# One start-up constant, the warming products and the unread products of a four-segment attention and feed-forward kernel

## The chip, the cores and the metric

The kernel runs on one core of one Trainium2 chip. Its time is the device time of one execution in microseconds (us). Five engines work side by side, each in its own order: TensorE (PE in the profile, its weight loads PEld), VectorE (DVE), ScalarE (ACT), GpSimd (POOL) and SyncE (SP, which issues most DMAs).

## The reference

The input x has 2048 rows of 512. Four layers follow each other: attention, feed-forward, attention, feed-forward, twice with the same weights, each added to x after a normalization.

```python
x = x + _A_ref(_layernorm(x), wq, wk, wv, wo, beta)
x = x + _B_ref(_layernorm(x), w_gate, w_up, w_down)
x = x + _A_ref(_layernorm(x), wq, wk, wv, wo, beta)
x = x + _B_ref(_layernorm(x), w_gate, w_up, w_down)
```

`_A_ref` has 32 heads of 16 columns and cuts the rows into 4 segments of 512. In a segment each head does a causal softmax attention (`a_dot`) and reads a memory matrix `M` with a normalizer `z` (`a_mem`), which gather phi(k) v and phi(k) over the earlier segments; phi(t) is t + 1 above zero and exp(t) below. The two are mixed by a gate for each head:

```python
g = sigmoid(beta).reshape(1, H, 1, 1)        # beta: 32 numbers
o = g * a_mem + (1.0 - g) * a_dot
```

`_B_ref` is `gelu(x @ w_gate) * (x @ w_up) @ w_down` with 1792 inner columns.

## The kernel before

The work is eight pieces, k = 0 to 7: four segments in each of the two attention layers, each with its feed-forward piece. All of x and all weights stay in SBUF. Rows lie on the 128 partitions, four tiles of 128 rows to a segment; the normalized rows are turned (`xnT`) by DMA transposes or, for some pieces, by TensorE transposes against an identity, and an engine evicts the turned tile from PSUM. Scores are computed with keys on the partitions, exponentiated by ScalarE (L1396) into one of ten slots `pt`, masked by GpSimd (L1343, L1348) or VectorE (L1353), and multiplied with the values (the flush, L954). The memory's update multiplies the turned `phik` with the values, and VectorE adds it to `macc` (L895).

The order of all instructions on all engines is written out by the kernel itself: `order` runs a model of the engines (`Clocks`, with a duration for each step) and emits each instruction where the model finds its inputs ready. TensorE's turn goes first to score rounds, then to an item (a group of products for one of the 8 PSUM banks). Where nothing is ready while scores are still to come, it emits an unread product of `warm`, a tile of ones, into a free bank: 128 weights by 512 columns, one instruction (through `product`, L476), or four with 32 weights each where the array is in its column tiling (L471). These are called fills here. The model counts each as `Clocks.MM[512]`, 0.2158 us. The fills beside some transposes (L584, 256 columns) are another piece of code.

The start is written by hand. Four tiles of x are loaded, two by SyncE's queue and two by ScalarE's, then beta on ScalarE's queue, spread to all 128 partitions (`beta_bc`, L315); SyncE loads the weights. TensorE begins with `WARM` unread products of 128 x 512 (`keep_warm`, L349), which keep it busy until the first data is there. The four tiles are normalized (VectorE L544) and turned by TensorE (`first_turn`, L596); ScalarE evicts the first two (L599), VectorE the other two (L601). Then follow the first k products (`first_k`, L909), two groups of q products (`first_q`, L914), the second k products, and their evictions (L1228, L1231, L1237 on ScalarE, L1234 on VectorE), and the first scores (L938).

From beta come two constants, exp(beta) in `tmp_e` (a corner of `macc`) and exp(-beta) in `tmp_e2`, both by ScalarE, which in its order stand after the statistics of the fourth tile and ahead of the evictions of L599:

```python
nc.scalar.activation(out=tmp_e, in_=beta_bc[:], func=ACT.Exp)                 # L1202
nc.scalar.activation(out=tmp_e2[:], in_=beta_bc[:], func=ACT.Exp, scale=-1.0) # L1203
```

VectorE adds one to each (`gate_constants`, L389, L391) after the eviction of L1234.

Of the kernel before, what the change touches and what calls it, by code (L numbers as in the profile page):

```python
# [11 lines left out]
ACT = mybir.ActivationFunctionType  # L12
# [3 lines left out]
BF16 = mybir.dt.bfloat16  # L16
I32 = mybir.dt.int32

P = 128
D = 512  # L20
H = 32
# [12 lines left out]
EPS_LN = 1e-5  # L34
EPS_MEM = 1e-6
MANUAL = {ENG.PE, ENG.Activation, ENG.SP, ENG.DVE, ENG.Pool}
WARM = 15
UNIT = 256
ROUNDS = 9
STEPS = KT * ROUNDS  # L40
# [17 lines left out]
BANKS = 8  # L58
# [227 lines left out]
def order(pol, nc, cst, seg, wrk, psp, A_x, A_wq, A_wk, A_wv, A_wo, A_beta, B_x, B_w_gate, B_w_up, B_w_down, out):  # L286
# [12 lines left out]
    wu_sb = cst.tile([P, KT, FF], BF16, name="wu_sb")  # L299
    wd_sb = cst.tile([P, FT, D], BF16, name="wd_sb")  # L300
    gel_sb = cst.tile([P, FT, L], BF16, name="gel_sb")
    beta_bc = cst.tile([P, H], BF16, name="beta_bc")

    def load(dst, src):
        nc.sync.dma_start(out=dst, in_=src)
# [6 lines left out]

    for j in range(TPS):
        (nc.scalar if j % 2 else nc.sync).dma_start(out=x_sb[:, j, :], in_=xv[:, j, :])
    nc.scalar.dma_start(out=beta_bc[:], in_=A_beta.partition_broadcast(P))  # L315
    for cols in (slice(0, D // 2), slice(D // 2, D)):
        load(w_att["k"][:, :, cols], w_view(A_wk)[:, :, cols])
        load(w_att["q"][:, :, cols], w_view(A_wq)[:, :, cols])
# [19 lines left out]
    warm = cst.tile([P, P], BF16, name="warm")  # L338
    wide = warm[:].unsqueeze(1).to_broadcast([P, 4, P])
# [4 lines left out]
    ps_all = psp.tile([P, BANKS, L], F32, tag="ps", bufs=1, name="ps")  # L344
    pt_all = wrk.tile([P, PT_SLOTS, 4, UNIT], BF16, tag="pt", bufs=1, name="pt")

    def keep_warm(n, bank):
        for _ in range(n):
            nc.tensor.matmul(ps_all[:, bank, :], lhsT=warm[:], rhs=wide, start=True, stop=True)  # L349

    keep_warm(WARM, 0)

# [23 lines left out]
    tmp_e2 = cst.tile([P, H], F32, name="tmp_e2")  # L376
    cden = cst.tile([P, H], BF16, name="cden")
    macc = cst.tile([P, 4, P], F32, name="macc")
    tmp_e = macc[:, 0, 0:H]
# [85 lines left out]
    def product(out, lhsT, rhs, start=True, stop=True):  # L465

        if ck.mode == "columns" or ck.mode == "rows" and (any(it.kind == "flush" and it.near() for it in items)):
            ck.tiling("columns")
            for c in range(4):
                r = slice(32 * c, 32 * c + 32)  # L470
                nc.tensor.matmul(out[r], lhsT=lhsT[:, r], rhs=rhs, start=start, stop=stop, tile_position=(0, 32 * c))  # L471
            ck.count += 4
        else:
            ck.tiling("whole")
            ck.count += 1
            nc.tensor.matmul(out, lhsT=lhsT, rhs=rhs, start=start, stop=stop)  # L476
# [722 lines left out]
    nc.scalar.activation(out=spare[:, 1, :], in_=x_sb[:, TPS - 1, :], func=ACT.Square, scale=root, bias=shift[:],  # L1199
                         accum_out=n0.mv[:, TPS - 1, 1:2])  # L1200

    nc.scalar.activation(out=tmp_e, in_=beta_bc[:], func=ACT.Exp)  # L1202
    nc.scalar.activation(out=tmp_e2[:], in_=beta_bc[:], func=ACT.Exp, scale=-1.0)  # L1203

    first_stats(0)
    first_stats(1)
# [14 lines left out]
    half = L // 2  # L1221
    n0.first_turn(0)
    n0.first_turn(1)
    n0.first_turn(2)
    n0.first_turn(3)
    ps1 = ps_all[:, 1, :]
# [47 lines left out]
    def next_e():  # L1274
        if not e_slots.free or e_slots.queue or phase[0] is not None:
            return
        now = streams[0][0] + streams[0][1] / STEPS if streams else 1e9
        act = ck.act
        idle = act.free <= ck.pe and act.table == "exp" and not act.only and not any(j[0] <= ck.pe and not j[4] for j in act.jobs)
        got = [j for j in e_jobs if j[1] <= ck.pe and j[2]() and (idle or j[0] <= now)]  # L1280
        if got:
            job = min(got, key=lambda j: j[0])
            e_jobs.remove(job)
            job[3](job[1], pol.e_slack)
            ck.serve()
# [17 lines left out]
    def tight():  # L1303

        return any(slot_free[slot_of(k, t)] is None for k, t in streams[2:4])
# [7 lines left out]
    def rounds_now(idle=False):  # L1313

        if not streams or phase[0] is not None and phase[1] > pol.hold or not rounds_ready(2):
            return 0
        n, left = len(free_pairs()), len(streams)
        wait = backlog()
        if n >= 2 and (idle or left <= 4 or wait < (pol.early if streams[0][0] < 1 else pol.starve)):
            return 2  # L1320
        return 0

    def pick():

        got = [i for i in range(BANKS) if banks[i] <= ck.pe]
        if not got:
            return None
        mine = sum(banks[i] > ck.pe for i in range(BANKS) if i not in score_banks)
        if streams and mine >= pol.cap and backlog() < pol.near and rounds_ready(2):
            return None  # L1330
        apart = {i for i in range(BANKS) if i not in score_banks and banks[i] > ck.pe + pol.soon} if streams else ()
        return min(got, key=lambda i: (-len(pairs_of(set(range(BANKS)) - {i, *apart})), banks[i]))

    def open_item(got, bank):
        it = min(got, key=lambda it: it.due())
        items.remove(it)
        it.ps.bank = bank
        banks[bank] = 1e9
        return it
# [83 lines left out]
    while streams or items or opened or ck.busy():  # L1423
        assert ck.pe < 2000.0, (streams[:1], [(it.kind, it.due()) for it in items[:9]], e_jobs[:2], banks)
        pol.move(ck.pe)
        ck.dve.shun = pol.shun
        ck.serve()
        next_e()
        n = rounds_now()
        if n:  # L1430
            score(n)
            continue
        if opened:
            cost, fn = opened.ops.pop(0)
            fn()
            ck.on_pe(cost)
            if not opened.ops:
                it, opened = opened, None
                it.done()
            continue  # L1440
        bank = pick()
        if bank is not None:
            late = ck.pe - pol.flush_wait
            for ck.back in (pol.lag, 0.0):
                got = [it for it in items if it.after in ev and it.ready() and (
                    it.kind != "flush" or not streams or tight() or it.posted < late or ck.mode == "columns")]
                if got:
                    break
            ck.back = 0.0
            if got:  # L1450
                opened = open_item(got, bank)
                continue

        n = rounds_now(True)
        if n:
            score(n)
            continue
        if bank is not None:
            if streams:
                ps = Psum()  # L1460
                ps.bank = bank
                product(ps(), warm[:], wide)
                ck.on_pe(Clocks.MM[512])
                ps.read(ck.pe)
                ck.fills.append(ck.pe)
                continue
        ck.pe += 0.05
        ck.stalls.append(ck.pe)
# [3 lines left out]
@with_exitstack  # L1472
def kernel(
    ctx: ExitStack,
    tc: tile.TileContext,
    A_x: bass.AP,
    A_wq: bass.AP,
    A_wk: bass.AP,
    A_wv: bass.AP,
    A_wo: bass.AP,  # L1480
    A_beta: bass.AP,
    B_x: bass.AP,
    B_w_gate: bass.AP,
    B_w_up: bass.AP,
    B_w_down: bass.AP,
    out: bass.AP,
):
    cst = ctx.enter_context(tc.tile_pool(name="cst", bufs=1))
    seg = ctx.enter_context(tc.tile_pool(name="seg", bufs=1))
    wrk = ctx.enter_context(tc.tile_pool(name="wrk", bufs=2))  # L1490
    psp = ctx.enter_context(tc.tile_pool(name="psp", bufs=1, space=bass.MemoryType.PSUM))
    ctx.enter_context(tc.manual_schedule(engines=MANUAL))
    order(Policy(POLICY, CHANGES), tc.nc, cst, seg, wrk, psp, A_x, A_wq, A_wk, A_wv, A_wo, A_beta, B_x, B_w_gate, B_w_up, B_w_down, out)
# [31 lines left out]
```

## Time and profile before

| what | value |
|---|---|
| time, median of 3 runs | 546.05 us (546.04 to 547.07) |
| the profiled execution | 545.75 us, span 544.0 us |
| TensorE busy | 531.3 us, 98% of the span |
| VectorE, ScalarE, GpSimd busy | 82%, 80%, 56% |
| mean granted TensorE clock | 0.999 |
| unread products at the start (L349) | 15 |
| fills (L476 and L471) | 19 instructions and 48 instructions |

The span runs from the first to the last instruction; the time has some work around it. In rows of the timeline the columns are start, duration, engine, line, operation, out<-in, count, and in brackets how long the engine was idle before and what ended that. A row of the chain of waits has start, duration and the work. In a table of stretches stand the bounds, the length, the busy time with the number of instructions, the granted TensorE clock, the DMA share and GB/s. The ends of matmuls are modelled, so a short idle time of TensorE can be hidden in the tail of the product before it.

### The profile page before, as it was taken

Reading aid. Unit: us, or ns where it says so; the run is one execution under the profiler, and the core shown is the slowest. Engines: PE = TensorE matmul, PEld = TensorE weight load, DVE = VectorE, ACT = ScalarE, POOL = GpSimd, SP = SyncE. Lnnn points to the kernel's source line nnn. Section 1 sums busy time; section 2 is a strip of 40 time slices with the busy share of each in tenths; the row PEclk is TensorE's granted clock in tenths of the full one; section 3 lists DMA queues with packets and bytes.
Section 4 is the critical chain, followed back from the end, with each engine's and each line's share of the span. In section 5 each row is a group of like instructions: output and inputs, shape, how many; then the busy total and the mean of one; then the engine's idle time right before and its main releaser. Section 6 shows DMA issues by size and latency. Waiting matters only on the chain.

```text
span 544.0 us, 21276 instructions
## 1 busy us (share of the span) xinstructions
PE 531.3 (98%) x9273; PEld 276.3 (51%) x9334; DVE 443.7 (82%) x816; ACT 434.7 (80%) x540; POOL 305.5 (56%) x359
## 2 busy tenths in 40 slices
PE   8999999999999999999999999999999999999997
PEld 4454555454545444554545555545465456555444
DVE  6998999799988999779987998889586797786342
ACT  5999989988898989989899798996879977920330
POOL 4898786369746788339993468716753265300000
PEclk9999999999999999999999999999999999999999
DMA  8406511610331123310312250221320114100001
GB/s 249 117 13 192 118 20 13 176 33 22 45 56 21 26 40 58 44 40 7 41 32 49 33 72 3 41 32 23 78 52 3 22 21 82 24 3 22 19 0 40
DMA packets 64926, 26.95 MB, mean 50 GB/s; under 512 B 49216, under 2 KB 64832, under 8 KB 64832
## 3 DMA queue, kind: packets, MB, share of 16 engines
q1 hardware_dynamic: 64400, 25.31, 22.6%
q8 instruction: 73, 1.20, 0.9%
q10 hardware_dynamic: 432, 0.27, 0.2%
q14 instruction: 21, 0.17, 0.1%
HBM read 9.71 MB, written 2.10 MB: 22 GB/s over the span
## 4 chain that ended last, share of the span: by engine, by line
PE 88%; DVE 7%; DMA 2%; issue 2%; ACT 0%; ACTq 0%; SPq 0%; DVEq 0%
PE ps L476 46%; PE ps L471 26%; PE ps L938 8%; PE ps L954 7%; DVE st L514 1%; DVE x_sb L1027 1%; DMA beta_bc<-in_A_beta_dram 1%; DVE byq L971 1%; PE ps L586 1%; DVE phiq L745 1%; PE ps L584 1%; DMA phik<-e 0%; DMA amT<-am 0%; DVE xn L544 0%; DVE e L764 0%
## 5 line engine op out<-in xcount | busy, mean ns | idle before, releaser
L1396 ACT ACTIVATE pt<-ps 128x1024 bf16<-128x1024 f32 x288 | 278.9, 1025 | 44.6 <-PE ps L938 41.1
L1343 POOL TENSOR_SCALAR_AFFINE_SELECT pt<-pt 128x256 bf16<-128x256 bf16 (+1 forms) x192 | 107.0, 571 | 118.0 <-ACT pt L1396 112.0
L1092 DVE TENSOR_TENSOR gel_sb<-gel_sb,ps 128x512 bf16<-128x512 bf16 x112 | 75.3, 682 | 33.9 <-PE ps L476 25.0
L476 PE MATMUL ps<-xnT,wu_sb 128*128 128x512 bf16 x287 | 66.8, 379 | 1.4 <-issue 1.1
L476 PE MATMUL ps<-xnT,wg_sb 128*128 128x512 bf16 x261 | 62.6, 379 | 0.9 <-issue 0.5
L764 POOL TENSOR_SCALAR e<-e 128x512 bf16<-128x512 bf16 x37 | 57.9, 1565 | 1.8 <-ACT e L741 0.7
L971 DVE STREAM_TRANSPOSE byq<-ps 128x512 f32<-128x512 f32 x64 | 45.0, 706 | 16.5 <-PE ps L954 15.9
L476 PE MATMUL ps<-wd_sb,gel_sb 128*128 128x512 bf16 (+1 forms) x293 | 56.8, 340 | 1.3 <-issue 1.0
L1348 POOL TENSOR_SCALAR_AFFINE_SELECT pt<-pt 64x1024 bf16<-64x1024 bf16 x40 | 47.8, 1196 | 15.0 <-ACT pt L1396 13.7
L1027 DVE TENSOR_TENSOR x_sb<-x_sb,ps 128x512 bf16<-128x512 bf16 (+1 forms) x68 | 42.8, 640 | 16.3 <-PE ps L476 14.7
L471 PE MATMUL ps<-wd_sb,gel_sb 128*32 128x512 bf16 (+1 forms) x792 | 47.1, 378 | 0.3 <-issue 0.3
L476 PEld LDWEIGHTS <-wu_sb 128*128 128x128 bf16 x301 | 28.2, 98 | 33.8 <-issue 0.7
L471 PE MATMUL ps<-xnT,wg_sb 128*32 128x512 bf16 x700 | 42.4, 380 | 0.0
L514 DVE BATCH_NORM_STATS2 st<-x_sb 128x6 f32<-128x512 bf16 x60 | 40.4, 674 | 0.4 <-DMA x_sb<-in_A_x_dram 0.3
L476 PEld LDWEIGHTS <-wg_sb 128*128 128x128 bf16 x273 | 25.3, 98 | 28.8 <-issue 0.2
L476 PEld LDWEIGHTS <-gel_sb 128*128 128x128 bf16 x306 | 28.3, 98 | 22.7 <-issue 1.1
L954 PE MATMUL ps<-pt,vaug 128*32 128x256 bf16 (+2 forms) x1344 | 34.6, 238 | 0.0
L417 POOL TENSOR_SCALAR kx<-kf,masks 128x512 bf16<-128x512 bf16 x20 | 33.5, 1678 | 1.2
L471 PE MATMUL ps<-xnT,wu_sb 128*32 128x512 bf16 x588 | 34.1, 379 | 0.0
L1151 ACT ACTIVATE gel_sb<-gel_sb 128x2048 bf16<-128x2048 bf16 (+1 forms) x21 | 33.2, 1643 | 0.0
L544 DVE TENSOR_SCALAR xn<-x_sb,mv,rs 128x512 bf16<-128x512 bf16 x58 | 31.3, 592 | 2.2 <-POOL rs L532 1.9
L954 PEld LDWEIGHTS <-vaug 128*32 128x32 bf16 x1344 | 27.8, 97 | 10.4 <-issue 2.2
(147 smaller groups left out, 883.6 us busy)
## 6 DMA issues: line engine op xcount, KB each, us to landing
vz<-vaug SPq DMA_DIRECT2D x14, 136.0 KB, 2.9
wg_sb<-in_B_w_gate_dram SPq DMA_DIRECT2D x8, 224.0 KB, 4.6
wu_sb<-in_B_w_up_dram SPq DMA_DIRECT2D x8, 224.0 KB, 4.3
wd_sb<-in_B_w_down_dram SPq DMA_DIRECT2D x7, 256.0 KB, 4.2
x_sb<-in_A_x_dram SPq DMA_DIRECT2D x3, 512.0 KB, 7.3
out_dram<-x_sb SPq DMA_DIRECT2D x12, 128.0 KB, 1.8
xnT<-xn SPq DMA_TRANSPOSE x40, 2.5
wk_sb<-in_A_wk_dram SPq DMA_DIRECT2D x2, 256.0 KB, 6.0
```

The lines of the kernel that those rows point to most:

```text
L471: nc.tensor.matmul(out[r], lhsT=lhsT[:, r], rhs=rhs, start=start, stop=stop, tile_position=(0, 32 * c))
L476: nc.tensor.matmul(out, lhsT=lhsT, rhs=rhs, start=start, stop=stop)
L514: nc.vector.bn_stats(out=self.st6[:, 0, :], in_=x_sb[:, self.tt0 + j, :])
L764: lambda eng: eng.tensor_scalar(out=e[0][:], in0=e[0][:], scalar1=1.0, scalar2=None, op0=ALU.min), summed)
L938: nc.tensor.matmul(ps_all[:, bank, o + c0:o + c0 + n], lhsT=lhsT, rhs=self.q[rows, b, q0:q0 + n], start=True, stop=True, tile_position=(32 ...
L954: nc.tensor.matmul(ps()[32 * j:32 * j + 32, q0:q0 + n], lhsT=va[:, ki * VW + g:ki * VW + g + 32], rhs=pt_all[:, places[i], j, c0:c0 + n], ...
L971: nc.vector.transpose(out=self.byq[:, par, :, :].rearrange("p a c -> p (a c)"), in_=ps()[:])
L1027: ck.dve.post(ck.made(), slack, (0.15 + 0.00104 * (c1 - c0), lambda: nc.vector.tensor_tensor(out=xt, in0=xt, in1=ps()[:, 0:c1 - c0], op=AL ...
L1092: ck.dve.post(ck.made(), NORMAL, (0.683, lambda: nc.vector.tensor_tensor(out=g, in0=g, in1=ps()[:], op=ALU.mult), lambda t: (ps.read(t), e ...
L1343: nc.gpsimd.affine_select(out=view, in_=view, pattern=[[0, 4], [0, n], [1, C]], compare_op=ALU.is_ge, fill=0.0, base=C, channel_multiplier=-1)
L1348: nc.gpsimd.affine_select(out=view, in_=view, pattern=[[0, 4 * TPS], [1, C]], compare_op=ALU.is_ge, fill=0.0, base=0, channel_multiplier=-1)
L1396: nc.scalar.activation(out=pt_all[:, s0:s0 + 2, 2 * p:2 * p + 2, :].rearrange("p r h c -> p h r c"), in_=ps_all[:, pair[0]:pair[1] + 1, :] ...
```

## The change

Beta is loaded as one row of 32 numbers in one partition. After the second tile's transposes, TensorE multiplies that row with one row of ones into the last PSUM bank, so that all 128 partitions get it, and ScalarE takes both exponentials from PSUM, now after the two evictions of L599 in its order. The warming products are 12 and not 15. A fill has 128 columns and not 512; the model of the engines still counts it as 512 columns, so that the order of all instructions and their banks stays what it was.

```diff
-WARM = 15
+WARM = 12
...
-    beta_bc = cst.tile([P, H], BF16, name="beta_bc")
+    beta_row = cst.tile([1, H], BF16, name="beta_row")
...
-    nc.scalar.dma_start(out=beta_bc[:], in_=A_beta.partition_broadcast(P))
+    nc.scalar.dma_start(out=beta_row[:], in_=A_beta.partition_broadcast(1))
...
-    nc.scalar.activation(out=tmp_e, in_=beta_bc[:], func=ACT.Exp)
-    nc.scalar.activation(out=tmp_e2[:], in_=beta_bc[:], func=ACT.Exp, scale=-1.0)
...
     n0.first_turn(0)
     n0.first_turn(1)
+    beta_ps = ps_all[:, BANKS - 1, 0:H]
+    nc.tensor.matmul(beta_ps, lhsT=warm[0:1, :], rhs=beta_row[:], start=True, stop=True)
+    nc.scalar.activation(out=tmp_e, in_=beta_ps, func=ACT.Exp)
+    nc.scalar.activation(out=tmp_e2[:], in_=beta_ps, func=ACT.Exp, scale=-1.0)
     n0.first_turn(2)
     n0.first_turn(3)
...
             if streams:
                 ps = Psum()
                 ps.bank = bank
-                product(ps(), warm[:], wide)
+                product(ps()[:, 0:P], warm[:], wide[:, 0, :])
                 ck.on_pe(Clocks.MM[512])
```

## The prediction

> **What bounds the kernel now.** I read the page first: how full the engines are, and which of them the chain that ended last runs through.
>
> ```profile
> span 544.0 us, 21276 instructions
> PE 531.3 (98%) x9273; PEld 276.3 (51%) x9334; DVE 443.7 (82%) x816; ACT 434.7 (80%) x540; POOL 305.5 (56%) x359
> PE 88%; DVE 7%; DMA 2%; issue 2%; ACT 0%; ACTq 0%; SPq 0%; DVEq 0%
> ```
>
> TensorE bounds the kernel and every other engine follows it, so a change must shorten a stretch in which TensorE itself is late. The edit touches two places: the start, and wherever unread products lie. For the start I read the chain of waits in order of time, then the timeline of the same microseconds.
>
> ```profile
> 1.71 5.38 DMA beta_bc<-in_A_beta_dram
> 7.09 0.02 issue
> 7.11 0.23 ACT macc L1202
> 7.34 0.12 ACT tmp_e L1203
> 7.46 0.98 ACT xnT L599 x2
> 8.44 0.04 issue
> 8.48 0.60 PE ps L909 x4
> ...
> 1.11 4.79 PE L349 MATMUL ps<-warm 128*128 128x512 bf16 x15 [1.11 <-DVE warm L340]
> 4.01 1.39 PEld L349 LDWEIGHTS <-warm 128*128 128x128 bf16 x7 [0.22 <-issue]
> 6.63 0.72 PE L596 MATMUL ps<-ident,xn 128*128 128x128 bf16 x8 [0.73 <-DVE xn L544]
> 7.16 0.73 DVE L544 TENSOR_SCALAR xn<-x_sb,mv,rs 128x512 bf16<-128x512 bf16 x2 [0.21 <-POOL rs L1193]
> 7.37 1.06 ACT L599 ACTIVATE xnT<-ps 128x512 bf16<-128x512 bf16 x2
> 7.63 0.72 PE L596 MATMUL ps<-ident,xn 128*128 128x128 bf16 x8 [0.29 <-DVE xn L544]
> 9.12 0.38 ACT L1228 ACTIVATE wd_sb<-ps 128x256 bf16<-128x256 f32 x1 [0.68 <-PE ps L909]
> 10.99 3.77 ACT L1396 ACTIVATE pt<-ps 128x1024 bf16<-128x1024 f32 x4 [0.18 <-PE ps L938]
> ```
>
> The chain begins with the load of beta. ScalarE's queue holds the two exponentials of beta ahead of the evictions of the first two turned tiles (L599), beta lands at 7.09, and the first k products (L909) wait for those evictions. Nothing needs beta so early; it is only queued first.
>
> For the unread products I read the groups that read `warm`, one row per form.
>
> ```profile
> L471 PE MATMUL ps<-warm x48: 377/379/380, 73.8 to 135.7; 128*32 128x512 bf16 x48
> L476 PE MATMUL ps<-warm x19: 376/379/390, 21.8 to 140.1; 128*128 128x512 bf16 x19
> ```
>
> An L471 product is four instructions side by side, so there are 48/4 + 19 = 31 fills, all between 21.8 and 140.1 us; for the last 400 us the kernel has none.
>
> **The change, part by part.** *Beta.* What leaves ScalarE's path is the wait for beta and the two exponentials. The next latest thing is TensorE's own turning. The first eight transposes (two tiles) run from 6.63 to 7.35; the second tile needs the second xn, so the first tile is done about 7.03. The evictions take 1.06 / 2 = 0.53 each and a little more for one alone: first from about 7.08, second from the end of the transposes at 7.35, or from 7.56 when ScalarE is free, to about 8.13 (now 7.37 + 1.06 = 8.43). But L909 also stands behind the fourth tile's transposes in TensorE's order: their xn is there at 7.16 + 0.73 = 7.89, four transposes at the pitch of 0.056 (below) issue from about 7.96 to 8.18. So L909 starts at about 8.20 and not at 8.48: **-0.28 us**.
>
> The product for beta goes between the second and the third tile's transposes, in TensorE's gap before 7.63, where it waits for xn. It has 32 columns and one row; its nearest row, a 128-column transpose, costs 0.056, so it hides unless beta lands after 7.5. Its load is one row instead of 128 on the same queue behind the same two x tiles, so I take 7.09 as the latest landing. Waiting behind it would be the third and fourth transposes, and everything after. The two exponentials now read PSUM, a form the trace lacks: between 0.12 (the chain's step for the second) and 0.38 each (L1228, eight times as wide, from PSUM). They stand after the evictions, at 8.13, and end by 8.4 to 8.9; the next in ScalarE's queue, L1228, can start only at 9.12 - 0.28 = 8.84, since it waited 0.68 for TensorE. I take nothing, with +0.05 as the bad end; without that cover it would be 0.2 to 0.8.
>
> *Warming.* Three products at the full-clock pitch: the last seven weight loads take 1.39, so (1.39 - 0.10) / 6 = 0.215 each, 0.65 in all. They end near 5.25 instead of 5.90, ahead of the first xn, for which TensorE already waits. Time: nothing; what it may cost is the clock (rivals).
>
> *Fills.* The pitch of 128 columns, and the fills with what surrounds them:
>
> ```profile
> 20.86 1.06 PE L586 MATMUL ps<-ident,xn 128*128 128x128 bf16 x16
> 21.31 1.62 ACT L462 ACTIVATE xnT<-ps 128x512 bf16<-128x512 bf16 x3
> 21.75 0.59 PE L476 MATMUL ps<-warm 128*128 128x512 bf16 x2
> ...
> 70.97 0.81 PE L476 MATMUL ps<-warm 128*128 128x512 bf16 x3
> 71.95 0.42 PEld L476 LDWEIGHTS <-phik 128*128 128x128 bf16 x7 [0.23 <-DMA phik<-e]
> ...
> 73.82 1.47 PE L471 MATMUL ps<-warm 128*32 128x512 bf16 x24
> 75.51 1.37 POOL L1343 TENSOR_SCALAR_AFFINE_SELECT pt<-pt 128x512 bf16<-128x512 bf16 x2
> 75.55 1.47 PE L476 MATMUL ps<-warm 128*128 128x512 bf16 x6
> 76.95 0.63 PE L954 MATMUL ps<-pt,vaug 128*32 128x256 bf16 x24
> ...
> 79.98 0.81 PE L476 MATMUL ps<-warm 128*128 128x512 bf16 x3
> 80.30 0.60 ACT L462 ACTIVATE xnT<-ps 128x512 bf16<-128x512 bf16 x1
> 81.29 1.89 PE L476 MATMUL ps<-xnT,wg_sb 128*128 128x512 bf16 x7
> ...
> 112.69 0.38 PE L476 MATMUL ps<-warm 128*128 128x512 bf16 x1
> 114.24 0.69 DVE L895 TENSOR_TENSOR macc<-macc,ps 128x512 f32<-128x512 f32 x1 [0.15 <-PE ps L476]
> ...
> 134.59 1.47 PE L471 MATMUL ps<-warm 128*32 128x512 bf16 x24
> 136.83 0.23 PEld L586 LDWEIGHTS <-xn 128*128 128x128 bf16 x4 [0.40 <-DVE xn L544]
> ```
>
> Sixteen transposes in 1.06 with a tail of 0.22 give a pitch of 0.84 / 15 = 0.056; six fills in 1.47 with a tail of 0.38 give 0.218. A cut fill saves 0.16, and 31 of them 5.0 us of TensorE time. A fill, though, stands where the order had nothing ready, so I ask at each group what the next real product waits for.
>
> - At 21.75, two fills: the v product needs the first eviction of 21.31, which lands about 21.9 (0.60 for one, as at 80.30); from 22.18 it can move to about 22.05. ScalarE has no idle time there. Between 0 and -0.13; I take -0.05.
> - At 70.97, three: the next products wait for the transposed phik at 71.95. Zero.
> - At 73.82 and 75.55, twelve: the flush at 76.95 needs the masks, which GpSimd ends at 75.51 + 1.37 = 76.88. The fills are long enough to hide in that; the 12 x 0.16 = 1.9 us become idle time. Zero.
> - At 79.98, three and one more before the gate products at 81.29: these need the eviction that ends at 80.90. Up to 81.29 - 80.95 = 0.34; ScalarE is busy here too, so I take half, -0.15.
> - At 112.69, one: the update behind it releases L895, for which VectorE waited 0.15. Up to -0.15; I take -0.07.
> - At 134.59, six: the transposes behind wait for xn, 0.40. Zero. The last three fills near 139 to 140 give at most 3 x 0.16 = 0.48 and probably a third of one; -0.05.
>
> After 141 us nothing changes any more, and what has been won up to there stays won.
>
> Sum: -0.28 - 0.05 - 0.15 - 0.07 - 0.05 = **-0.60 us**; by the ends of the terms from about -0.25 to -1.35. The profiled execution took 545.75 (544.0 and 1.75 around it), 0.30 under the median of 546.05; against the median I forecast 546.05 - 0.6 = **545.45**.
>
> **The rivals.** *The clock falls at the start (slower).* The granted clock in stretches of 3.41 us, and just after the last:
>
> ```profile
> 3.94:7.35 3.41, 2.67 (x17) 1.00 0.78 212
> 539.83:543.24 3.41, 1.04 (x10) 1.00 0.14 39
> 543.20:543.40 0.20, 0.00 (x0) 0.61 0.00 0
> ...
> 8.92 1.04 PE L914 MATMUL ps<-xnT,wq_sb 128*128 128x256 bf16 x8
> 9.79 0.60 PE L909 MATMUL ps<-xnT,wk_sb 128*128 128x256 bf16 x4
> ```
>
> A stretch busy for 1.04 of 3.41 (30%) ended with the clock cut; one busy for 2.67 (78%) did not. With three products fewer the latter falls to 2.67 - 0.65 = 2.02 (59%). If the clock is cut for less than some share between 59% and 78%, it is cut at 7.35 for one stretch, to 10.77. Price: sixteen products of 256 columns, pitch (1.04 - 0.27) / 7 = 0.11; at half clock from about 8.5 ten of them are done by 10.77, six more take 0.66, so they issue until 11.4, where now the last group ends its issue at 9.79 + 0.44 = 10.23. That is +1.2 against before; less the 0.32 of the fills, 546.05 + 0.9 = **546.9**. Stretches with the cut fills could fall too: twelve of them leave 3.41 - 1.9 = 1.5 (44%) if a stretch begins at 73.7; that would push it beyond 547.2. For it: two of the edits take activity away. Against it: 59% is far from 30%.
>
> By the Trainium skill, "TensorE: Matmul & The Clock Gate", Part 1, the clock is halved only after a whole idle window of about 3.4 us; by that nothing would fall here, and the sum would stand. The trace does not bear it out exactly: the clock went at 543.2 at the end of a stretch that was 30% busy. Part 4 of the same page says that transposes do not count as activity in the same way; by that the first stretch is emptier than its busy time, which makes this rival likelier.
>
> *The fills pass whole (faster).* The chain of waits counts TensorE through the fills at 73.8 to 76.95. If my reading of the masks is wrong and the flush can move, up to 1.9 us more come out: 545.45 - 1.9 = **543.6**. Against it: 76.88 and 76.95 fit too well.
>
> *Beta still holds the start (no change).* If the one-row load lands no earlier and TensorE, not ScalarE, now stands at it past 7.6, the 0.28 is lost again and what remains is the fills: **545.7**, or 546.0 if those are absorbed as well.
>
> **How the numbers follow.** My forecast 0.58, the clock 0.20, the fills whole 0.10, beta 0.12. A measurement of this kernel can tell about 0.2% (1.1 us) from no change, so faster means under 544.95 and slower over 547.15. Faster: the fills whole, 0.10, and the far end of my terms, 0.10, together 0.20. Slower: the half of the clock's chance in which more than one stretch falls, or the fills give nothing back, 0.10, and 0.05 for a stall that I have not seen: 0.15. Within: 0.65. The range runs from my terms' good end, 546.05 - 1.35 = 544.7, to one fall of the clock with little from the fills, 547.0; beyond lie the fills whole and a second fall.
>
> **What would show it.** Right: the two L599 evictions begin near 7.1 and L909 near 8.2; the exponentials of beta stand between them and L1228, which waits for TensorE and not for them; L938's first scores start near 10.3 instead of 10.56. The flush now at 76.95 waits idle for GpSimd, and the update's phik still ends the wait near 71.7. The granted clock is 1.00 from 4 to 543 us. Wrong: a granted clock of half anywhere between 7 and 15 or 73 and 82 us, shown as a doubled pitch of L909 and L914; a wait of TensorE for beta ahead of the third tile's transposes; a time under 544.7 or over 547.0.

## The result and the profile after

| | before | changed |
|---|---|---|
| median of 11 runs | 545.86 us (545.50 to 547.07) | 544.78 us (544.50 to 545.29) |
| ratio | | 0.9978, 95% interval 0.9971 to 0.9986 |
| span of the profiled execution | 544.0 us | 543.0 us |

The change makes the kernel 0.22% faster, some 1.1 us, where 0.6 were forecast. The page of the changed kernel:

```profile
span 543.0 us, 21272 instructions
PE 527.9 (97%) x9271; PEld 276.1 (51%) x9332; DVE 443.4 (82%) x816; ACT 434.5 (80%) x540; POOL 306.4 (56%) x359
PE 83%; DVE 11%; issue 2%; DMA 2%; ACT 1%; POOL 0%; SPq 0%; ACTq 0%; DVEq 0%
```

TensorE lost 3.4 us of work but the span only 1.0 us, and 4% of the chain went to VectorE: most of what was cut is now waiting time. The start, from the chain of waits (start, duration, what) and then from the timeline of the changed kernel:

```profile
1.23 3.00 DMA x_sb<-in_A_x_dram
...
7.40 0.72 PE ps L596 x8
8.12 0.44 PE ps L909 x4
...
3.23 1.29 DVE L1183 BATCH_NORM_STATS2 st<-x_sb 128x6 f32<-128x512 bf16 x2 [0.60 <-DMA x_sb<-in_A_x_dram]
6.83 1.08 ACT L599 ACTIVATE xnT<-ps 128x512 bf16<-128x512 bf16 x2 [1.01 <-PE ps L596]
7.05 0.18 PE L1223 MATMUL ps<-beta_row,warm 1*128 1x32 bf16 x1
7.80 0.20 ACT L1224 ACTIVATE macc<-ps 128x32 f32<-128x32 f32 x1
7.97 0.60 PE L909 MATMUL ps<-xnT,wk_sb 128*128 128x256 bf16 x4
8.60 0.38 ACT L1230 ACTIVATE wd_sb<-ps 128x256 bf16<-128x256 f32 x1 [0.51 <-PE ps L909]
```

Beta has left the chain, which now begins with a tile of x. The evictions (L599) start right behind the transposes, the product for beta (L1223) stands in a gap, its exponentials end before TensorE has work for L1230, which waits 0.51 for TensorE. The first k products start at 7.97, not at 8.48: 0.51 earlier, of which VectorE's first statistics, at 3.23 and not at 3.45, make 0.22.

The places of the fills in the timeline:

```profile
73.07 0.64 PE L471 MATMUL ps<-warm 128*32 128x128 bf16 x24
74.22 0.40 PE L938 MATMUL ps<-q,kf 16*128 16x64 bf16 x10 [0.37 <-ACT pt L1398]
74.54 0.51 PE L476 MATMUL ps<-warm 128*128 128x128 bf16 x6
74.82 1.38 POOL L1345 TENSOR_SCALAR_AFFINE_SELECT pt<-pt 128x512 bf16<-128x512 bf16 x2
74.98 0.51 PE L954 MATMUL ps<-pt,vaug 128*32 128x256 bf16 x16
75.84 0.30 PE L954 MATMUL ps<-pt,vaug 128*32 128x64 bf16 x8 [0.34 <-POOL pt L1345]
...
79.96 1.24 PE L476 MATMUL ps<-xnT,wg_sb 128*128 128x512 bf16 x4
...
108.85 2.37 SPq L437 DMA_TRANSPOSE phik<-e  x1
112.37 0.96 PE L476 MATMUL ps<-vaug,phik 128*128 128x128 bf16 x13 [0.41 <-DMA phik<-e]
113.44 0.69 DVE L895 TENSOR_TENSOR macc<-macc,ps 128x512 f32<-128x512 f32 x1 [0.49 <-PE ps L476]
```

The flush (L954) begins at 74.98, while the two masks run until 74.82 + 1.38 = 76.20, and goes on at 75.84, when only the first of them is done: asked for alone, the row is a mask of 128x512 that takes 0.97, until 75.79, and a shorter one of 128x256 that ends at 76.20. The gate products moved from 81.29 to 79.96. At 112 us the shorter fill only lengthens the wait for the turned phik.

To see where time was won I compare the same exponentiations of scores (288 of them, in the same order) in the profiled executions: how much earlier (-) or later (+) one starts than in the profile before, in us. The column heads are its start before.

| kernel | 11.0 | 29.2 | 70.1 | 78.5 | 86.8 | 114.8 | 169.9 | 470.3 |
|---|---|---|---|---|---|---|---|---|
| changed | -0.52 | -0.69 | -0.69 | -0.99 | -1.13 | -0.80 | -1.06 | -1.01 |
| changed, once more | -0.39 | -0.56 | -0.56 | -0.85 | -0.99 | -0.32 | -1.21 | -0.84 |
| fills alone | -0.18 | -0.35 | -0.35 | -0.64 | -0.79 | -0.60 | -0.86 | -0.52 |
| twelve fills alone | -0.13 | -0.13 | -0.13 | -0.42 | -0.42 | +0.17 | -0.44 | -0.14 |
| all but these twelve | -0.39 | -0.56 | -0.57 | -0.45 | -0.60 | -0.30 | -0.57 | -0.32 |
| start alone | -0.43 | -0.44 | -0.44 | -0.41 | -0.41 | +0.04 | -0.08 | +0.11 |
| beta alone | -0.14 | -0.15 | -0.15 | +0.08 | +0.08 | +0.48 | +0.37 | +0.36 |
| warming alone | -0.29 | -0.29 | -0.29 | +0.09 | +0.08 | +0.27 | +0.15 | -0.01 |

From one column to the next a row shows what that stretch gave. One execution has chance in it: where DMAs end the wait (near 72, 112 and 400 us) the rows move by some tenths whatever was edited.

### The profile page after: what moved, and what is told of

It reads as the page before. It is cut to its first block, busy times and chain, and to the rows that moved or that the text cites. A ratio compares the mean times of both kernels' runs of the same rounds, so it can differ in the third digit from the quotient of the medians.

```text
span 543.0 us, 21272 instructions
## 1 busy us (share of the span) xinstructions
PE 527.9 (97%) x9271; PEld 276.1 (51%) x9332; DVE 443.4 (82%) x816; ACT 434.5 (80%) x540; POOL 306.4 (56%) x359
## 4 chain that ended last, share of the span: by engine, by line
PE 83%; DVE 11%; issue 2%; DMA 2%; ACT 1%; POOL 0%; SPq 0%; ACTq 0%; DVEq 0%
PE ps L476 44%; PE ps L471 25%; PE ps L938 7%; PE ps L954 6%; DVE st L514 2%; DVE x_sb L1027 1%; DVE xn L544 1%; DVE byq L971 1%; DMA phik<-e 1%; DVE phiq L745 1%; DMA x_sb<-in_A_x_dram 1%; DVE mv L522 1%; DMA amT<-am 0%; DVE e L745 0%; ACT pt L1398 0%
## 5 line engine op out<-in xcount | busy, mean ns | idle before, releaser
L1345 POOL TENSOR_SCALAR_AFFINE_SELECT pt<-pt 128x256 bf16<-128x256 bf16 (+1 forms) x192 | 108.3, 577 | 116.5 <-ACT pt L1398 110.6
L954 PE MATMUL ps<-pt,vaug 128*32 128x256 bf16 (+2 forms) x1344 | 34.8, 238 | 0.3 <-POOL pt L1345 0.3
L954 PEld LDWEIGHTS <-vaug 128*32 128x32 bf16 x1344 | 27.9, 97 | 10.5 <-issue 2.3
```

The source lines that it names most:

```text
L954: nc.tensor.matmul(ps()[32 * j:32 * j + 32, q0:q0 + n], lhsT=va[:, ki * VW + g:ki * VW + g + 32], rhs=pt_all[:, places[i], j, c0:c0 + n], ...
L1345: nc.gpsimd.affine_select(out=view, in_=view, pattern=[[0, 4], [0, n], [1, C]], compare_op=ALU.is_ge, fill=0.0, base=C, channel_multiplier=-1)
```

## The experiments

All ratios are to the kernel before, run on the same chip in the same rounds; each row of the table above belongs to one of these kernels.

**Beta alone.**

```diff
-WARM = 12
+WARM = 15
-                product(ps()[:, 0:P], warm[:], wide[:, 0, :])
+                product(ps(), warm[:], wide)
```

> The kernel before with the beta part alone (one row, product, exponentials behind the two evictions); 15 warming products and 512-column fills stay. Theory 'landing' (the 128 small rows of beta delay the x tiles; without them the first normalized tile is there 0.23 us sooner, and the queue order gives the other 0.29): VectorE's first statistics at about 3.23 instead of 3.45, first k products at about 7.97 instead of 8.48, the whole start and the end 0.5 us earlier, 545.4. Rival 'chance' (tiles land 0.2 us earlier or later from one execution to the next, whatever is loaded): statistics near 3.45, first k products near 8.20, 0.3 us in all, 545.6. Rival 'clock' (the earlier start came from fewer warming products): first k products after 8.3, no gain.

Measured: 546.04 us, ratio 1.0000 (0.9991 to 1.0009). Its timeline:

```profile
3.60 1.29 DVE L1183 BATCH_NORM_STATS2 st<-x_sb 128x6 f32<-128x512 bf16 x2 [0.97 <-DMA x_sb<-in_A_x_dram]
8.34 0.60 PE L909 MATMUL ps<-xnT,wk_sb 128*128 128x256 bf16 x4
```

The x tiles landed late in this execution although beta was a single row: "landing" with its 0.23 falls, "chance" fits. From first statistics to first k products it is 4.74, as in the changed kernel, where the profile before has 8.48 - 3.45 = 5.03. So 0.29 of the start's 0.51 is the queue order; the rest was the draw.

**The late exponentials alone**, with beta still loaded to 128 partitions.

```diff
-    nc.scalar.activation(out=tmp_e, in_=beta_bc[:], func=ACT.Exp)
-    nc.scalar.activation(out=tmp_e2[:], in_=beta_bc[:], func=ACT.Exp, scale=-1.0)
...
     n0.first_turn(1)
+    nc.scalar.activation(out=tmp_e, in_=beta_bc[:], func=ACT.Exp)
+    nc.scalar.activation(out=tmp_e2[:], in_=beta_bc[:], func=ACT.Exp, scale=-1.0)
```

> The kernel before with only the two exponentials of beta moved behind the two evictions in ScalarE's order; beta is still loaded to 128 partitions. 'Landing': the tiles land as before (statistics at 3.45), only the order helps: first k products at about 8.20, 0.28 us earlier, 545.6. 'Chance': the same on average, but the statistics may begin anywhere from 3.2 to 3.5. If the single row itself and not the order were what counts: no gain, 8.48.

Measured: 546.22 us, ratio 1.0001 (0.9992 to 1.0010).

```profile
1.50 5.77 PE L349 MATMUL ps<-warm 128*128 128x512 bf16 x14
7.11 1.43 PE L596 MATMUL ps<-ident,xn 128*128 128x128 bf16 x16
8.67 0.60 PE L909 MATMUL ps<-xnT,wk_sb 128*128 128x256 bf16 x4
```

The 0.28 did not show, for a reason that none of the theories had: here the full clock came only at 6.72 us (3.94 in the profile before), the 15 warming products lasted until 7.27, and the transposes started behind them at 7.11, not behind xn. What the order gives, late warming took.

**Fills alone.**

```diff
-                product(ps(), warm[:], wide)
+                product(ps()[:, 0:P], warm[:], wide[:, 0, :])
```

> The kernel before with 128-column fills alone. Theory 'first mask' (the flush at 76.95 waits for the first of the two masks only, so the twelve fills ahead of it do hold TensorE): the exponentials run 0.15 us ahead after 22 us, 0.45 after 76 us, 0.6 after 90 us, some of that is lost at the turned phik near 110 us, 0.5 us in all, 545.4. Theory of the prediction (masks at 76.88 pin the flush): 0.05 ahead until 80 us, 0.2 after 90 us, 0.3 in all, 545.55.

Measured: 545.05 us, ratio 0.9983 (0.9974 to 0.9992): most of the whole gain. The row of the table has the steps that "first mask" expects: -0.17 after 22 us, -0.29 at 76, -0.15 by 87. With the beta of before, its start was as short as that of the changed kernel:

```profile
3.56 1.29 DVE L1183 BATCH_NORM_STATS2 st<-x_sb 128x6 f32<-128x512 bf16 x2 [0.93 <-DMA x_sb<-in_A_x_dram]
6.87 0.23 ACT L1202 ACTIVATE macc<-beta_bc 128x32 f32<-128x32 bf16 x1 [0.92 <-DMA beta_bc<-in_A_beta_dram]
8.30 0.60 PE L909 MATMUL ps<-xnT,wk_sb 128*128 128x256 bf16 x4
```

8.30 - 3.56 = 4.74: the exponentials of beta could start at 6.87 and not at 7.11, x landed later, and ScalarE was through with them at about the time at which the first tile was turned. So the wait for beta costs between 0 and 0.29, by the draw.

**Warming alone.**

```diff
-WARM = 15
+WARM = 12
```

> The kernel before with 12 warming products instead of 15, nothing else. All theories but one: TensorE still waits for the first xn, first k products at 8.48, 545.9, no difference over 0.1 us. Rival 'clock at the start': granted clock halved in a stretch between 7 and 12 us, first scores 1 us later, 546.9.

Measured: 546.33 us, ratio 1.0003 (0.9994 to 1.0011); the full clock was kept. No difference, as the sum had it.

**Six warming products** in the changed kernel.

```diff
-WARM = 12
+WARM = 6
```

> The changed kernel with 6 warming products instead of 12. They end at 3.7 us even at half clock, ahead of the first xn at 6.4, so TensorE has 2.7 us of nothing. Theory 'full clock is granted after a stretch of 3.41 us that is busy by some share between 64% and 83%' (from the grants seen so far at 3.94 and 6.72 us): no stretch reaches that until TensorE is dense from 8 us on, so the full clock comes between 10 and 14 us, the products of first k and first q have a pitch of 0.21 instead of 0.11, and the time rises by 1 to 3 us, to 545.8 to 547.8. Rival 'any busy stretch will do, the transposes are enough': no difference, 544.8.

Measured: 546.84 us, ratio 1.0015 (1.0006 to 1.0024), 2 us above the changed kernel. Stretches of its trace (bounds, length, TensorE busy, granted clock, DMA):

```profile
0.45:3.86 3.41, 2.74 (x6) 1.00 0.54 165
3.86:7.28 3.42, 0.73 (x9) 1.00 1.07 291
7.28:10.69 3.41, 3.24 (x20) 0.50 1.03 337
10.69:14.10 3.41, 3.08 (x38) 1.00 0.86 283
```

The size came out, but not the way I wrote: the full clock was granted at 3.86, after a stretch 80% busy, and taken back at 7.28, after one that was 21% busy, for exactly one stretch. (The first row's 1.00 is a stretch without a record; its products have the half-clock pitch.) This is the first rival of the prediction, with its place and its price: the first scores' exponentials start at +1.03 against -0.52, 1.55 us for one stretch, where 1.2 was worked out. That holds for the profiled execution and, by their mean clock of 0.996 or 0.997, for four others; the other five of the ten had 0.999 or 1.000 and took 546.03 to 548.30 all the same. A full clock that comes late, as the expectation had it, does not show in that mean; no trace of these five was kept, so how they lost their time is open.

**No fills, order not kept.**

```diff
-                product(ps()[:, 0:P], warm[:], wide[:, 0, :])
```

> The changed kernel with the unread products between the items left out altogether (nothing else in the order moves). Theory 'fills hold TensorE only where its next input is already there': another 31 x 0.056 = 1.7 us of TensorE time goes, of which the part after 21, 76 and 140 us counts: 0.1 to 0.3 us faster than the changed kernel, 544.5 to 544.7. Rival 'clock': with the 12 fills at 73 to 76 us gone a stretch there falls under the share at which the clock is cut, TensorE runs at half for 3.4 us, 546 or more.

Measured: 553.58 us, ratio 1.0140 (1.0126 to 1.0154).

```profile
137.20:140.62 3.42, 0.81 (x24) 1.00 0.00 0
140.62:144.03 3.41, 2.15 (x54) 0.50 0.02 5
144.03:147.45 3.42, 3.42 (x39) 0.50 0.00 0
```

Two things went together. Leaving out the call also leaves out the model's step for the array's tiling, so the planned order of all engines changed from 70 us on; and after a stretch with 0.81 us of work the clock was halved for two stretches. How much each took this run cannot say exactly. Two stretches at half clock can cost at most half their length, 3.4 us (an estimate from these rows), of the 7.4 us above the kernel before. Without **the 256-column fills** too:

```diff
-            ops = [(Clocks.MM[512] / 2, whole(lambda: nc.tensor.matmul(
-                ps()[:, half:L], lhsT=warm[:], rhs=wide[:, 0:2, :], start=True, stop=True)))] * fill
+            ops = [(Clocks.MM[512] / 2, whole(lambda: None))] * fill
```

> As the changed kernel without the fills between the items, and also without the 256-column fills beside the transposes at 77 to 80, 136 to 140 and 498 us (24 x 0.107 = 2.6 us of TensorE time). If these stand on the path as the chain of waits has it at 78 to 80 us: another 0.3 to 0.5 us faster than without the first kind alone, near 544.2. If the transposes wait for VectorE's xn anyway: no difference.

Measured: 552.89 us, ratio 1.0129 (1.0114 to 1.0145), with the same changed order; what those fills are worth stays open. The clock was now also halved after the former fills beside the transposes:

```profile
76.49:79.90 3.41, 2.37 (x65) 1.00 0.02 5
79.90:83.32 3.42, 3.11 (x17) 0.50 0.00 0
```

**All but the twelve fills at 76 us, and these twelve alone.** In the changed kernel, as shown, and in the kernel before, with the two branches exchanged:

```diff
+                if 5 <= len(ck.fills) < 17:
+                    product(ps(), warm[:], wide)
+                else:
+                    product(ps()[:, 0:P], warm[:], wide[:, 0, :])
```

> The changed kernel with the twelve fills ahead of the flush at 76 us at 512 columns again, the other nineteen at 128. Theory 'first mask': these twelve alone are worth 0.3 us, so 0.3 slower than the changed kernel, 545.1, with the exponentials after 76 us 0.3 later and those before it unmoved. Theory of the prediction (masks pin the flush): no difference, 544.8.

> The kernel before with only the twelve fills ahead of the flush at 76 us at 128 columns. Theory 'first mask': 0.3 us faster than before (545.8 against 546.1), exponentials unmoved before 75 us and 0.3 earlier from 78 us on. Theory of the prediction: no difference. Above 0.8 us: these twelve are the whole gain.

Measured: with all but the twelve 545.31 us, ratio 0.9987 (0.9978 to 0.9996); with the twelve alone 545.58 us, ratio 0.9995 (0.9986 to 1.0003). The intervals leave the twelve between 0 and about 0.8 us. The profiles are sharper. From 70.1 to 78.5 all four rows in which the twelve are short gain 0.29 or 0.30, and the four in which they are long gain nothing, losing 0.03 to 0.38. The timeline with the twelve alone:

```profile
75.38 1.38 POOL L1343 TENSOR_SCALAR_AFFINE_SELECT pt<-pt 128x512 bf16<-128x512 bf16 x2
75.68 0.52 PE L954 MATMUL ps<-pt,vaug 128*32 128x256 bf16 x16
76.40 0.30 PE L954 MATMUL ps<-pt,vaug 128*32 128x64 bf16 x8 [0.20 <-POOL pt L1343]
77.55 0.27 PE L938 MATMUL ps<-q,kf 16*128 16x64 bf16 x5 [0.28 <-DVE macc L893]
```

The masks are at 75.38 + 1.38 = 76.76, the flush goes on at 76.40 all the same; the first mask, asked for alone, ends at 76.35, and the second is by the kernel that of the next group of heads. The next thing that pins TensorE is VectorE's copy of macc at 77.55, and it caps the gain at 0.3. For the flush, "first mask" stands.

The 0.3 is there before the flush, however. First the profile before, then the twelve alone:

```profile
75.22 0.40 PE L938 MATMUL ps<-q,kf 16*128 16x64 bf16 x12
75.51 0.96 POOL L1343 TENSOR_SCALAR_AFFINE_SELECT pt<-pt 128x512 bf16<-128x512 bf16 x1
75.74 1.94 ACT L1396 ACTIVATE pt<-ps 128x1024 bf16<-128x1024 f32 x2 [0.30 <-PE ps L938]
76.43 0.45 POOL L1343 TENSOR_SCALAR_AFFINE_SELECT pt<-pt 128x256 bf16<-128x256 bf16 x1
...
74.92 0.40 PE L938 MATMUL ps<-q,kf 16*128 16x64 bf16 x10 [0.38 <-ACT pt L1396]
75.41 1.94 ACT L1396 ACTIVATE pt<-ps 128x1024 bf16<-128x1024 f32 x2
```

Behind the first six fills stand not the flush but the scores of 75.22, for which ScalarE waited 0.30; with short fills these scores wait for ScalarE instead. Compared as in the table, from the exponentiation at 73.9 to the one at 75.7 the four rows with short fills gain 0.27, the four others nothing. That the flush could move as well kept this gain. No run shortens one six without the other, so the division between them is read from the profiles, not tested.

**No fills, order kept.** The steps of the model stay, only the product goes.

```diff
-                product(ps()[:, 0:P], warm[:], wide[:, 0, :])
+                if ck.mode == "columns" or ck.mode == "rows" and (any(it.kind == "flush" and it.near() for it in items)):
+                    ck.tiling("columns")
+                    ck.count += 4
+                else:
+                    ck.tiling("whole")
+                    ck.count += 1
```

> The changed kernel without the 31 fills between the items, this time with the steps of the model kept that go with a fill, so that all other instructions keep their order. Theory 'fills hold TensorE': the rest of their time goes as well, about 0.2 us faster than the changed kernel, 544.6, the full clock granted throughout. Rival 'clock': the stretch of 3.41 us that holds the former fills near 73 to 77 or 134 to 138 us falls under about a third busy, the clock is halved for the next one, and the time is 1 us or more above the changed kernel. Rival 'order': the 7 us of the earlier version without fills came from fewer products, not from its other order: 552 again.

Measured: 545.18 us (544.12 to 546.25), ratio 0.9987 (0.9978 to 0.9996). The 7 us of the first version without fills are gone, so that time went with its other order, the lost clock included. The runs are spread over 2.1 us, where the changed kernel's lie within 0.8; the profiled one was the fastest of all executions, with a span of 542.4 and the full clock kept. The mean granted clock of each execution says what parts them: the six from 544.12 to 545.18 had 1.000, the five from 545.63 to 546.25 had 0.997 or 0.994, and one stretch of 3.41 us at half clock lowers the mean by 0.003. Where the clock fell in these five is not known, since none of them was profiled. With the full clock this kernel is no slower than the changed one (544.34 to 545.18 in its repeated run, with a mean clock of 0.999 or 1.000 throughout). So fills of 128 columns are the better choice of the two, and no version here beat the changed kernel in the median.

**The start alone, and the changed kernel once more.**

```diff
-                product(ps()[:, 0:P], warm[:], wide[:, 0, :])
+                product(ps(), warm[:], wide)
```

> The changed kernel with all fills at 512 columns again: beta's row, the late exponentials and 12 warming products alone. If the start is worth what the two profiled executions differ by (0.5 us): 545.6. If its gain is a chance of when the x tiles land and when the clock rises: 546.0 to 546.1, no difference from before over 0.2 us; the step from VectorE's first statistics to the first k products is 4.74 us instead of 5.03.

> The changed kernel once more, on the same chip as the three others. 1.1 us faster than before (545.0 against 546.1). Its profile shows how far the times at which the x tiles land and the turned phik lands move without any change: statistics between 3.2 and 3.65 us, the turned phik near 72 and 112 us within 0.4 us.

Measured: the start alone 545.59 us, ratio 0.9992 (0.9983 to 1.0000), its step from first statistics to first k products 4.79; the changed kernel 544.84 us, ratio 0.9978 (0.9969 to 0.9988), as before. Beta and warming together bring between 0 and 0.9 us, the fills 0.4 to 1.4 by their own run. The repeated profile has its first statistics at 3.35 and its row differs from the first one by up to 0.5 at 114.8 us, with nothing changed.

## Why the prediction was wrong

The direction and the range held; the sum, -0.60, was about half of what was measured (0.9978 of 546.05 is 1.2 us less). By its steps:

- **The start, -0.28.** The mechanism and the size were right for this execution: 5.03 to 4.74 from first statistics to first k products, that is -0.29; the -0.22 beside it are x tiles that landed earlier, most likely by chance: first statistics start at 3.22 to 3.60 in the nine profiles with one row of beta and at 3.33 to 3.64 in the five with 128, so a small shift is not excluded. What I did not see is that the profile before showed the wait for beta at its largest: with the old order the step is 5.03, 4.74, 4.82 and 5.02 in four profiles (before, fills, warming and the twelve alone). On the median the runs do not size it: 0.9992 (0.9983 to 1.0000) with the warming, 1.0000 (0.9991 to 1.0009) for beta alone.
- **Warming, 0.** Right (1.0003). It has a use that I left out: where the full clock comes late, 15 products hold the first transposes (7.11 in the run with the late exponentials).
- **The twelve fills at 73.8 and 75.6, 0.** This is the step that failed: I asked of all twelve only what the flush waits for, and read the flush as pinned. The first six stand ahead of the scores at 75.22, for which ScalarE waited 0.30, and 0.27 is won there. And the flush was not pinned: I read "75.51 1.37 ... x2" as one end, at 76.88. The row holds two masks; the last eight of the flush's first 24 products need the first, which ends 0.41 earlier, at 76.47, and the other sixteen ran during that mask with the twelve alone. The match of 76.88 and 76.95 was chance. The twelve are worth 0.30 in the profile, capped by VectorE's macc, and on top they take up the DMA's delay near 72 us, at which the kernels with long fills lost 0.03 to 0.38.
- **The fills at 21.75, -0.05.** Mis-sized: -0.17 in every row with short fills there. I had ScalarE, which is never idle there, hold most of the 0.13 that I allowed at most; it held nothing of that.
- **The fills at 80, -0.15.** Right: -0.14 or -0.15 in the four rows in which they are short.
- **The fill at 112.7, -0.07.** Zero: phik lands later than the fill ends (0.41 of idle). The profile before was fortunate there: nearly every later one loses 0.2 to 0.7 between 109 and 115 us.
- **The fills from 134 on, -0.05.** The six at 134.6 were misread in the same way: they stand ahead of scores, and the exponentiation behind them, at 136.5, starts 0.27 earlier in the four rows with these fills short and not at all earlier in the others. By 144 three of the four keep 0.15 of it. The fourth, and the twelve alone with these fills long, gain more by then, for a reason that no run separates.
- **Together.** With 0.29 for the start, the profiles give 0.29 + 0.17 + 0.30 + 0.14 + 0.15 = 1.05, against 0.60; most of the difference is the twelve fills that I put at nothing, 0.30.
- **The rivals.** The clock did not fall with 12 products: the first stretch behind the grant, 2.50 of 3.41 busy, kept it.

```profile
4.76:8.17 3.41, 2.50 (x23) 1.00 1.04 310
73.01:76.42 3.41, 2.69 (x100) 1.00 0.02 5
```

It does fall with 6, for one stretch, at 1.55 us. The Trainium skill, "TensorE: Matmul & The Clock Gate", Part 1, has the clock taken back after an idle window; here stretches with 0.73, 0.81 and 1.04 us of work of 3.41 lost it, so a window need not be idle. "The fills pass whole" was right in its mechanism and too large in its price: with the twelve alone the flush begins at 75.68 and not at 76.95, but of the 1.9 only 0.3 comes out behind it.

## What to carry to other kernels

A row of a profile that counts two instructions has two ends: before a wait is called pinned, split the row and ask which of them the waiter needs. Of each group of fillers ask what stands right behind it, and who waits for that. Filler work that keeps TensorE's clock need not be as long as the gap that a planner foresees; a shorter one that keeps the clock lets the real inputs decide, while none at all lost the clock in five of eleven executions. A wait at the start that ends with a DMA is a draw: one profile shows one draw, and its size is not what the median pays.

## What was not expected

- The edge of the granted clock moves from execution to execution, though all five begin with the same warming products: the full clock came at 3.94, 4.02, 6.72, 4.47 and 5.06 us in the profile before and in the first four experiments.
- Busy time alone does not say when the clock is taken back: 2.37 of 3.41, with the former fills missing among the transposes, lost it; this stretch, of the kernel with no fills and its order kept, with 2.06, did not:

```profile
69.26:72.67 3.41, 2.06 (x30) 1.00 0.41 43
```

That transposes count for less would explain it; no run here separated that.
- The issue of the same transposing DMA of phik took 1.19 us in eight of twelve profiles near 110 us and 2.04 to 2.37 in the other four.
